# Inverting two blocks of a chunked delta rule as a pair, with their key products issued in the head of the kernel

## The chip, the cores and the metric

The kernel runs on one core of a Trainium2 chip. The metric is device microseconds of one execution; lower is better. The engines are named as the profile names them: PE (TensorE matmul) and PEld (its weight loads), DVE (VectorE), ACT (ScalarE), POOL (GpSimd) and SP (SyncE, which here only issues DMAs).

## The reference, cut to what matters

```python
# q, k, v: (4, 8, 768, 48), beta: (4, 8, 768); all float32
# w_in (384, 2048), w_out (2048, 384): 64-bit floats
k_n = k / (np.linalg.norm(k, axis=-1, keepdims=True) + 1e-06)
state = np.zeros((B, H, D, D))
for t in range(S):                       # S = 768 tokens, one after the other
    kt, vt, bt = k_n[:, :, t], v[:, :, t], beta[:, :, t, None]
    y[:, :, t] = einsum('bhd,bhde->bhe', q[:, :, t], state)
    v_old = einsum('bhde,bhd->bhe', state, kt)
    state = state + bt[:, :, :, None] * einsum('bhd,bhe->bhde', kt, vt - v_old)
x = y.transpose(0, 2, 1, 3).reshape(B * S, H * D)     # 3072 tokens of 384
h = x @ w_in
return np.maximum(0.01 * h, h) @ w_out
```

A recurrence over the tokens (a delta rule, with a 48x48 state per head) is followed by a two-layer feed-forward network on its output.

## The kernel before, in words

The 768 tokens are cut into 12 blocks of 64 (`C`). Within a block the recurrence is solved in closed form: a Gram matrix of the block's keys is made on PE, the inverse of the triangular system that it gives is worked out, and small matmuls with that inverse give the outputs and the new state. All 32 heads of the 4 sequences go together, in two groups `g`.

**The inverse.** `inv` inverts two 32x32 triangles (the halves of a block) per head and sequence on DVE, in 31 elimination steps (`eliminate`, L381): each step is a multiply into `tmp` (L391) and a subtract from `T` (L396), each in two parts `x`, so four instructions and two independent chains. `NB` (L93) says which blocks share one inverse. Blocks 0 and 1 are inverted together, with 128 partitions holding two blocks by two halves by 32 problems (`two`); every later block alone, with the same 64 problems held twice and each copy working on half of the rows of `T`. For a single block, `T` and a transposed copy `Tt` (L456) go to DRAM (`td`, `tt`) and come back as block-diagonal operands `A` and `B` (tile `sq`, L468 and L472) for the products `pz` and `pu` that join the two halves (`merge_z`, `merge_u`).

**The Gram products.** `gram(n)` loads a block's keys and queries (tile `kq`, two buffers), issues on PE products of 64 keys with 64 keys and 64 queries at once (tile `pg`, L308), copies the key part to SBUF on ACT (`gs`), sends it through DRAM (`gd`) into the layout of the inverse (`L`, L346), masks the query part on DVE (L325) and copies the corner of the key part on DVE (`gm`, L333).

**The solve.** `solve(n)` runs through slots: `merge_z`, `merge_u`, `kt` (tile `pk`), `step_w` (`pw`), `step_y` (`py`), the state (`pc`).

**The feed-forward network.** `ffn(n)` has 16 steps `f` per block: a first product (`ph`, L759), an activation on ACT, and a second product into `po` (L750), two steps behind. In block 0 it is one product of float32; from block 1 on in three products of a high and a low part: `xh`, `xl` of its input, `gh`, `gl` of its hidden values (`gl` on DVE, L774), and a high and a low part of the weights.

**The weights** come in as eight pieces `wr` (`load_w`, 1.5 MB each) of 64-bit floats; ACT and DVE make 32-bit floats of them in block 0, from bit fields: `pack` (ACT L152), `conv` (four DVE instructions, L162 to L165), `expand` (ACT L172), `final` (DVE L179). Then `cast` (ACT L186) makes the high part and `lows` (DVE L193) the low part. Piece `j` serves the steps `f` = 2j and 2j + 1. The tiles of pieces 3 and 4 are later those of `A` and `B` (tags c3, c4).

**The order.** The main loop goes block by block and step by step; the tuples `IV`, `GG`, `G4` and `SV` say at which steps of a block the instructions of the inverse, of the Gram products and of the solve for the next blocks are put into the program, and the table `work` does so for the weights. A scheduler then orders each engine's queue at compile time by a model of the times. `behind(name)` keeps an instruction behind a marked one of the same engine. On the chip every queue runs in its fixed order. Block 0's inputs for the solve are fetched by `fetch(0, g)` on SP, between weight pieces 1 and 2; 16 matmuls without use (`warm`, L398) run on PE late in the first inverse.

The lines that place the parts named above:

```python
NB = [[0, 1]] + [[n] for n in range(2, nblk)]                     # L93
for f in range(KA): load_w(f)                                     # L836: pieces 0, 1
for g in range(NGR): fetch(0, g)                                  # L838
for f in range(KA, WEARLY): load_w(f)                             # L840: pieces 2, 3
NF + 0: ((lows, 3),), NF + 1: ((lows, 4),),                       # L875, block 1's steps
NF + 2: ((lows, 5),), NF + 3: ((lows, 6),), NF + 5: ((lows, 7),)  # L876
```

## Time and profile before

| | us |
|---|---|
| median of 3 runs | 609.85 |
| lowest and highest of them | 608.66, 611.44 |
| the profiled execution: its own time | 607.1 |
| its span in the trace | 605.3 |
| PE busy in the span | 564.8 |

The stages can be read from the start of the first `ph` product of each block: the head is 0 to 53.3 us, block 0 is 53.3 to 114.8 us, block 1 is 114.8 to 171.2 us, block 2 is 171.2 to 216.2 us, and a later block takes about 44.2 us. A busy share is an average; what a stage is worth is seen in its own rows, and the wait that ended last there says which engine sets its end.

### The profile page before, as it was taken

Reading aid. Unit: us, or ns where it says so; the run is one execution under the profiler, and the core shown is the slowest. Engines: PE = TensorE matmul, PEld = TensorE weight load, DVE = VectorE, ACT = ScalarE, POOL = GpSimd, SP = SyncE. Lnnn points to the kernel's source line nnn. Section 1 sums busy time; section 2 is a strip of 40 time slices with the busy share of each in tenths; the row PEclk is TensorE's granted clock in tenths of the full one; section 3 lists DMA queues with packets and bytes.
Section 4 is the critical chain, followed back from the end, with each engine's and each line's share of the span. In section 5 each row is a group of like instructions: output and inputs, shape, how many; then the busy total and the mean of one; then the engine's idle time right before and its main releaser. Section 6 shows DMA issues by size and latency. Waiting matters only on the chain.

```text
span 605.3 us, 22381 instructions
## 1 busy us (share of the span) xinstructions
PE 564.8 (93%) x9146; PEld 518.2 (86%) x9146; DVE 448.7 (74%) x1981; ACT 311.3 (51%) x786; POOL 77.8 (13%) x135
## 2 busy tenths in 40 slices
PE   5287989889899999999999999999999999999996
PEld 4266767678799999999999999999999999999996
DVE  3999899978848969859859869769779679341221
ACT  3287976744546446436445445445445445454432
POOL 7000000100140040040130130130120210210100
PEclk9987999999999999999999999999999999999999
DMA  5994942244290273381481490490491450410100
GB/s 124 303 286 174 341 95 60 51 86 83 83 187 8 50 118 109 65 182 32 72 181 23 74 194 9 78 195 16 67 195 29 73 123 2 83 34 3 28 1 27
DMA packets 104423, 59.69 MB, mean 99 GB/s; under 512 B 92544, under 2 KB 93632, under 8 KB 103296
## 3 DMA queue, kind: packets, MB, share of 16 engines
q1 hardware_dynamic: 99168, 50.32, 37.5%
q0 software_dynamic: 4576, 7.22, 5.4%
q8 instruction: 72, 1.18, 0.9%
q10 hardware_dynamic: 576, 0.72, 0.6%
q14 instruction: 31, 0.25, 0.2%
HBM read 46.96 MB, written 11.27 MB: 96 GB/s over the span
## 4 chain that ended last, share of the span: by engine, by line
PE 73%; DVE 16%; DMA 4%; issue 3%; ACT 2%; SPq 1%; DVEq 0%; POOL 0%; ACTq 0%
PE po L750 30%; PE ph L759 29%; DVE tmp L391 3%; DVE T L396 3%; PE pw L656 3%; PE py L693 3%; PE pg L308 2%; DVE w L193 2%; DMA tt<-T 2%; PE pk L631 2%; DVE cg L179 2%; PE pc L631 1%; PE px L728 1%; DVE rq L325 1%; DMA sq<-tt 1%
## 5 line engine op out<-in xcount | busy, mean ns | idle before, releaser
L759 PE MATMUL ph<-xh,w 128*128 128x256 f32 x1056 | 203.9, 284 | 0.0
L750 PE MATMUL po<-w,gh 128*128 128x384 f32 x704 | 180.0, 345 | 0.0
L769 ACT ACTIVATE gh<-ph 128x256 fp32r<-128x256 f32 (+1 forms) x192 | 73.5, 385 | 202.6 <-PE ph L759 121.2
L759 PEld LDWEIGHTS ph<-xh,w 128*128 128x128 f32 x1056 | 168.1, 188 | 2.7 <-issue 2.0
L774 DVE TENSOR_TENSOR gl<-ph,gh 128x256 fp32r<-128x256 f32 x176 | 74.3, 423 | 108.4 <-ACT ph L773 103.3
L759 PE MATMUL ph<-xl,w 128*128 128x256 f32 x528 | 148.4, 283 | 1.8 <-DVE xl L128 1.8
L750 PEld LDWEIGHTS po<-w,gh 128*128 128x128 f32 x704 | 120.2, 188 | 3.7 <-issue 1.4
L750 PE MATMUL po<-w,gl 128*128 128x384 f32 x352 | 112.9, 339 | 2.4 <-DVE gl L774 2.4
L396 DVE TENSOR_TENSOR T<-T,tmp 128x60 f32<-128x60 f32 (+35 forms) x661 | 110.8, 207 | 0.7
L391 DVE TENSOR_TENSOR tmp<-T,L 128x60 f32<-128x60 f32 (+35 forms) x661 | 110.8, 208 | 0.6
L759 PEld LDWEIGHTS ph<-xl,w 128*128 128x128 f32 x528 | 99.5, 188 | 2.6 <-DVE xl L128 2.2
L750 PEld LDWEIGHTS po<-w,gl 128*128 128x128 f32 x352 | 65.3, 188 | 3.2 <-DVE gl L774 3.1
L773 ACT ACTIVATE ph<-ph 128x256 f32<-128x256 f32 x176 | 67.0, 380 | 0.0
L468 POOL DMA_DIRECT2D sq<-tt x32 | 18.9, 596 | 281.3 <-PE po L750 97.9
L801 POOL DMA_DIRECT2D out<-ob x44 | 23.3, 533 | 140.1 <-ACT ob L800 138.1
L325 DVE TENSOR_TENSOR rq<-pg,csb 64x256 f32<-64x256 f32 x80 | 33.7, 422 | 3.0 <-ACT gs L312 1.4
L642 ACT ACTIVATE rt<-pk 48x512 f32<-48x512 f32 x44 | 26.0, 592 | 4.4 <-PE pk L631 3.6
L759 PE MATMUL ph<-x,cg 128*128 128x256 f32 x96 | 22.8, 386 | 4.0 <-DVE cg L179 2.4
L759 PEld LDWEIGHTS ph<-x,cg 128*128 128x128 f32 x96 | 17.7, 190 | 8.9 <-DVE cg L179 4.1
L658 ACT COPY rv<-pw 64x384 f32<-64x384 f32 x48 | 22.7, 474 | 3.6 <-PE pw L656 2.4
L647 DVE TENSOR_TENSOR rv<-rv,nt 64x384 f32<-64x384 f32 x44 | 23.2, 551 | 1.4 <-ACT nt L589 0.6
L693 PEld LDWEIGHTS py<-rv,rq 128*32 128x32 f32 x1536 | 19.4, 114 | 5.6 <-ACT rv L658 2.0
(108 smaller groups left out, 620.8 us busy)
## 6 DMA issues: line engine op xcount, KB each, us to landing
wr<-in_w_all SPq DMA_DIRECT2D x8, 1536.0 KB, 13.4
kq<-in_kqT SPq DMA_DIRECT2D x40, 192.0 KB, 6.7
rk<-in_kv SPq DMA_DIRECT2D x24, 192.0 KB, 5.3
rv<-in_kv SPq DMA_DIRECT2D x24, 192.0 KB, 6.0
rq<-in_qT SPq DMA_DIRECT2D x24, 192.0 KB, 3.4
L<-gd SPq DMA_DIRECT2D x18, 256.0 KB, 4.2
out<-ob POOLq DMA_DIRECT2D x44, 96.0 KB, 5.0
td<-T SPq DMA_DIRECT2D x20, 128.0 KB, 3.3
```

The lines of the kernel that those rows point to most:

```text
L325: nc.vector.tensor_tensor(qa[to, c, b * NPAIR:(b + 1) * NPAIR], pv[b][r, 1], tri[r].rearrange("p (o t) -> p o t", o=1).broadcast_to([C, NP ...
L391: nc.vector.tensor_tensor(tv, t[:, :, j:j + 1].broadcast_to([P, k, w]), L[:, j, j + 1:].rearrange("p (o w) -> p o w", o=1).broadcast_to([P ...
L396: mark["steps"] = nc.vector.tensor_tensor(t, t, tv, ALU.subtract).ins
L642: nc.scalar.mul(ts[g][STATE[g], c], pv[g][c * C:c * C + D].rearrange("p (y v) t -> p y v t", y=2), -1.0)
L647: nc.vector.tensor_tensor(v[to, :, us], v[to, :, us], nt[to, g, :, us].rearrange("p h (u o) -> p h u o", o=1).broadcast_to([C, 2, NPAIR, D ...
L693: nc.tensor.matmul(pv[a:a + HC, u * D:(u + 1) * D], qa[:, c, u, e * HC:(e + 1) * HC], v[:, c, u], start=True, stop=True)
L750: i = nc.tensor.matmul(po[t][:, :DO], a[:, ts_], w, start=(f == 0 and k == 0), stop=(f == NFC - 1 and k + 1 == len(ways)))
L759: i = nc.tensor.matmul(ph, w[:, cc * P:(cc + 1) * P], a, start=(k == 0), stop=(k + 1 == len(ways)))
L769: i = nc.scalar.activation(gh, ph, AF.Prelu, alpha=0.01)
L773: i = nc.scalar.activation(ph, ph, AF.Prelu, alpha=0.01)
L774: mark["gl"] = nc.vector.tensor_tensor(gl, ph, gh.bitcast(F32), ALU.subtract).ins
L801: nc.gpsimd.dma_start(out[r0:r0 + C], ob[a:a + C])
```

## The change

- Blocks 2 and 3 are inverted together, as blocks 0 and 1 are. The 31 steps of this pair are put into block 0 (steps 9 to 17, where block 2's own stood); block 1 gets no inverse.
- The key-with-key products of blocks 2 and 3 (`ahead`) are issued in the head, between the first inverse's preparation and its steps, 64 columns wide. Block 2's keys come with its whole `kq` load, which moves ahead of the weights; block 3's keys alone come by four DMAs on POOL into a corner of the tile of weight piece 7 (`ahead_loads`). ACT copies the products out; 16 DMAs on POOL write `gd` and 8 more write the corner parts to DRAM (`gc`). `arrive`, at step 3 of block 0, reads them back into `L` and `gm` with four DMAs on POOL; the corner copies of DVE are gone for these two blocks.
- The key-with-query products of blocks 2 and 3 and their masks stand in block 1 (steps 4 and 5, and 10 and 11); the masks of block 2 stay behind both chains of the inverse. Block 3's `kq` load stays behind the `B` operand of block 2.
- Block 0's fetches go ahead of all weight pieces; `pack` 0 to 2 stay behind the scaling of block 0's `v`.
- `lows` 3 to 7 go to steps 0, 3, 5, 7, 9 of block 1 in place of 0, 1, 2, 3, 5, and stay behind the last steps of both chains of the pair's inverse (before: behind one of them).
- `A` and `B` of block 3 are filled after block 2's `pu` has read them (`fill`); `T` of a pair goes to DRAM by one DMA per block and array.
- `solve(2)` in block 1 starts at step 7 in place of 4.

```diff
-    NB = [[0, 1]] + [[n] for n in range(2, nblk)]
+    NB = [[0, 1], [2, 3]] + [[n] for n in range(4, nblk)]
...
     def lows(j):
...
-        with behind("dv"), behind("el2" if j > 2 else None):
+        with behind("gl" if j > 3 else "dv"), behind("el0" if j > 2 else None), behind("el1" if j > 2 else None):
             after(nc.vector.tensor_tensor(lo, g, hi.bitcast(F32), ALU.subtract))
...
+    def products(n, g, ps, keys, x, gate=None):
+        w = x.stop - x.start
+        for p in range(NPAIR):
+            for c in range(2):
+                for b in range(2):
+                    r = slice(b * R0, b * R0 + D)
+                    with behind(gate):
+                        nc.tensor.matmul(ps[b][c * 64:(c + 1) * 64, p * w * C:(p + 1) * w * C],
+                                         keys[r, c ^ b, p, 0], kqs[n][g][r, c ^ b, p, x].rearrange("p x t -> p (x t)"),
+                                         start=True, stop=True)
...
+    def ahead_loads():
+        load_kq(pair[0], "kq")
+        t = corner["sb"] = sb.tile([P, 8 * DO], F32, tag="w7", name="k3", bufs=1)
...
+        for g in range(NGR):
+            for b in range(2):
+                nc.gpsimd.dma_start(
+                    keys[b * R0:b * R0 + D, g].rearrange("p s u x t -> p (s u) (x t)"),
+                    kqT[pair[1], g, b].rearrange("d (m x t) -> d m x t", x=2, t=C)[:, :, 0])
+
+    def ahead(n):
...
+        pv = [products(n, g, [t[:, g * h:(g + 1) * h] for t in ps], ks[g], slice(0, 1)) for g in range(NGR)]
...
+        for g in range(NGR):
+            for b in range(2):
+                nc.scalar.copy(gs[:, g, b], pv[g][b][:, 0])
+            grams_out(nc.gpsimd, gd, gs[:, g], g)
+            for c in range(2):
+                nc.gpsimd.dma_start(gc[2 * g + c].rearrange("p u t -> p u t"),
+                                    gs[c * 64:c * 64 + HC, g].rearrange("p b u t -> p (b u) t")[:, :, HC:])
+
+    def arrive():
...
+            nc.gpsimd.dma_start(Lh[b0][i * 64:(i + 1) * 64].rearrange("l j i -> l (j i)"), gd.rearrange("l j i -> l (j i)"))
...
+            nc.gpsimd.dma_start(gm[n], corner[n][1].rearrange("k p u t -> (k p) u t"))
+
+    def gram(n):
+        if n in pair:
+            if n != pair[0]:
+                load_kq(n, "B")
...
+            pv = [products(n, g, [t[:, g * h:(g + 1) * h] for t in ps], kqs[n][g], slice(1, 2), "ph") for g in range(NGR)]
+            for g in range(NGR):
+                masked(n, g, [t[:, 0] for t in pv[g]], *(("el0", "el1") if n == pair[0] else ("gl",)))
+                yield
+            return
...
+                    if two:
+                        nc.scalar.copy(Tt.rearrange("p i (x m) -> p m x i", x=2), T.rearrange("p (m x) i -> p m x i", x=2))
...
+                        if two:
+                            nc.sync.dma_start(tt, Tt[i * 64:i * 64 + HS])
+                            nc.sync.dma_start(rows, T[i * 64:i * 64 + 64])
+                            continue
...
+                    fill(NB[b][0])
...
-                    mark["el2"] = mark["steps"]
+                    mark["el0"], mark["el1"] = mark["step0"], mark["step1"]
...
+            if n == NB[1][0]:
+                fill(NB[1][1])
...
-    for f in range(KA):
-        load_w(f)
     for g in range(NGR):
         fetch(0, g)
-    for f in range(KA, WEARLY):
+    ahead_loads()
+    for f in range(WEARLY):
         load_w(f)
     signs()
     next(fg)
+    weave(1, (iv, 2, 0, 1))
+    for n in pair:
+        ahead(n)
     for j in range(NPACK):
-        pack(j)
-    weave(1, (iv, NI, 0, 1))
+        pack(j, "vs")
+    weave(1, (iv, NI - 2, 0, 1))
...
-        3: ((expand, 3, "h0_3"),),
+        3: ((expand, 3, "h0_3"), (arrive,)),
...
-        NF + 0: ((lows, 3),), NF + 1: ((lows, 4),),
-        NF + 2: ((lows, 5),), NF + 3: ((lows, 6),), NF + 5: ((lows, 7),)}
+        NF + 0: ((lows, 3),), NF + 3: ((lows, 4),),
+        NF + 5: ((lows, 5),), NF + 7: ((lows, 6),), NF + 9: ((lows, 7),)}
...
-IV, GG = ((9, 17), (6, 17), (2, 12), (2, 12)), ((2, 4), (1, 2))
+IV, GG = ((9, 17), (6, 17), (2, 12), (2, 12)), ((4, 5), (10, 11))
...
-SV = (1, 2, 4, 5, 7, 8, 9), (4, 6, 7, 9, 11, 12), (2, 4, 5, 7, 9, 10, 14), (3, 5, 6, 8, 10, 11, 14)
+SV = (1, 2, 4, 5, 7, 8, 9), (7, 8, 9, 11, 13, 14), (2, 4, 5, 7, 9, 10, 14), (3, 5, 6, 8, 10, 11, 14)
```

## Rows read from the trace of the kernel before

**Rows 1.** Busy time by stage: window, then engines, PE clock, DMA share, GB/s.

```profile
37.40:53.30 15.90, 11.93 (x394) 9.93 (x393) 14.74 (x21) 10.55 (x22) 0.00 (x0) 0.68 0.59 124
...
70.00:89.50 19.50, 17.11 (x228) 12.13 (x220) 18.73 (x30) 16.10 (x26) 0.00 (x0) 1.00 0.65 168
89.50:114.80 25.30, 24.18 (x395) 18.04 (x395) 24.91 (x128) 19.66 (x31) 0.00 (x0) 1.00 0.21 50
114.80:129.00 14.20, 10.01 (x114) 8.31 (x113) 14.04 (x32) 6.47 (x17) 2.21 (x4) 1.00 0.25 48
...
150.00:171.20 21.20, 19.21 (x461) 17.64 (x461) 18.21 (x112) 11.73 (x28) 3.54 (x6) 1.00 0.45 97
...
260.80:305.00 44.20, 44.20 (x732) 41.55 (x731) 35.79 (x177) 21.73 (x60) 5.59 (x11) 1.00 0.48 94
```

**Rows 2.** Waits of PE in block 0 (us, times, longest): the longest.

```profile
PE ph L759 <- DVE cg L179: 2.4, 1, 2.4
```

**Rows 3.** Waits of PE in block 1: the three longest.

```profile
PE po L750 <- DVE gl L774: 2.4, 2, 1.4
PE pc L668 <- issue: 1.9, 1, 1.9
PE ph L759 <- DVE xl L128: 1.8, 2, 1.2
```

**Rows 4.** Chain that ended last, block 0: ends of an unbroken DVE stretch.

```profile
70.36 1.76 DVE w L193
...
87.83 1.65 DVE cg L179
```

**Rows 5.** Timeline of DVE: block 2's masks, corners, inverse; low parts of the weights.

```profile
74.22 1.75 DVE L325 TENSOR_TENSOR rq<-pg,csb 64x256 f32<-64x256 f32 x4
...
76.00 0.58 DVE L333 COPY gm<-gs 32x256 f32<-32x256 f32 x2
...
99.93 0.28 DVE L391 TENSOR_TENSOR tmp<-T,L 128x31 f32<-128x31 f32 x2
...
118.95 6.75 DVE L193 TENSOR_TENSOR w<-cg,w 128x1536 fp32r<-128x1536 f32 x4
...
129.66 0.17 DVE L396 TENSOR_TENSOR T<-T,tmp 128x8 f32<-128x8 f32 x1
```

**Rows 6.** Timeline of DVE in the head: first and last step of the first inverse.

```profile
16.79 0.28 DVE L391 TENSOR_TENSOR tmp<-T,L 128x31 f32<-128x31 f32 x2
...
37.14 0.19 DVE L396 TENSOR_TENSOR T<-T,tmp 128x16 f32<-128x16 f32 x1
```

**Rows 7.** Timeline of ACT: scaling of block 0's v; transposed copy of T.

```profile
29.91 7.40 ACT L595 ACTIVATE rv<-rv,nt 64x48 f32<-64x48 f32 x32
...
129.87 1.11 ACT L456 COPY T<-T 128x512 f32<-128x512 f32 x1 [0.30 <-DVE T L396]
```

**Rows 8.** Timeline of PE: small products and the matmuls without use.

```profile
17.18 2.16 PE L264 MATMUL ph<-qx,kx 48*64 48x64 f32 x58
...
31.87 6.72 PE L403 MATMUL warm<-neg 128*128 128x512 f32 x16
...
69.51 1.10 PE L308 MATMUL pg<-kq 48*64 48x128 f32 x32
...
139.92 0.64 PE L501 MATMUL pz<-sq,gm 128*32 128x128 f32 x16 [0.55 <-DMA sq<-tt]
```

**Rows 9.** Chain that ended last, last block: two feed-forward steps without a wait.

```profile
572.29 2.13 PE ph L759 x18
574.42 2.11 PE po L750 x12
```

**Rows 10.** Groups of POOL: DMA issues of the Gram products.

```profile
L316 POOL DMA_DIRECT2D gd<-gs x8 | 4.7, 593 | 50.5 <-ACT gs L312 45.9 <-issue 4.2 <-ACT xh L127 0.4
```

**Rows 11.** The page's groups (busy, mean ns) and DMA issues (us to landing).

```profile
L774 DVE TENSOR_TENSOR gl<-ph,gh 128x256 fp32r<-128x256 f32 x176 | 74.3, 423 | 108.4 <-ACT ph L773 103.3
...
kq<-in_kqT SPq DMA_DIRECT2D x40, 192.0 KB, 6.7
```

More of the change, by code (lines that the diff above doesn't have):

```diff
@@ new lines, in grams_out, with masked @@
+    def grams_out(queue, gd, gs, g):
+        for c in range(2):
+            for e in range(2):
+                a = e * HS + g * GH + c * GU
+                queue.dma_start(
+                    gd[a:a + GU].rearrange("l j i -> j l i"),
+                    gs[c * 64 + e * HC:c * 64 + (e + 1) * HC].rearrange("p b u t -> p (b u) t")[:, :, e * HC:(e + 1) * HC])
+    def masked(n, g, pq, *gates):
+        qa, to = of("q", n, g), DATA[g]
+        for b in range(2):
+            for c in range(2):
+                r = slice(c * 64, (c + 1) * 64)
+                with ExitStack() as gate:
+                    for x in gates:
+                        gate.enter_context(behind(x))
+                    nc.vector.tensor_tensor(
+                        qa[to, c, b * NPAIR:(b + 1) * NPAIR], pq[b][r],
+                        tri[r].rearrange("p (o t) -> p o t", o=1).broadcast_to([C, NPAIR, C]), ALU.mult)
@@ L331, in corners @@
                     k = 2 * g + c
-                    with behind("gl") if n > 2 else nullcontext():
+                    with behind("gl"):
                         nc.vector.tensor_copy(gm[n][k * HC:(k + 1) * HC].rearrange("p (b u) t -> p b u t", b=2), gs[c * 64:c * 64 + HC, :, :, HC:])
-            if n == 2:
-                masked()
-                corners()
-            elif not g:
-                masked()
+            if not g:
+                masks()
                 held.append(corners)
             else:
-                tails.extend([[masked], held + [corners]])
+                tails.extend([[masks], held + [corners]])
                 held.clear()
@@ L394, in eliminate @@
             parts.append((tv, t[:, :, j + 1:]))
-        for tv, t in parts:
-            mark["steps"] = nc.vector.tensor_tensor(t, t, tv, ALU.subtract).ins
+        for x, (tv, t) in enumerate(parts):
+            mark["steps"] = mark[f"step{x}"] = nc.vector.tensor_tensor(t, t, tv, ALU.subtract).ins
     def warm(x, count):
@@ L413, in inv @@
         T = X[:, 0:M * HC].rearrange("p (m i) -> p m i", m=M)
-        if two:
+        if not b:
             nc.gpsimd.memset(T, 0.0)
@@ L485, in place, with fill @@
                 half_of(n, g, e), Tts[n][0][a:a + HC].rearrange("p (y g u) i -> p g y u i", y=2, g=NGR)[:, g])
+    def fill(n):
+        td, tt = Tts[n]
+        A, B = square(0), square(1)
+        queue = nc.gpsimd if n > NS else nc.sync
+        for k in range(4):
+            r = slice(k * HC, (k + 1) * HC)
+            mark["A"] = queue.dma_start(A[r, :, r], tt[k * GU:(k + 1) * GU].rearrange("u i m -> i u m")).ins
+        for v in range(4):
+            r = slice(v * HC, (v + 1) * HC)
+            with behind("A" if n > NS else None):
+                mark["B"] = queue.dma_start(B[r, :, r], td[1, v::4].rearrange("l m i -> m l i")).ins
     squares = {}
```

127 lines of the change are left out of this document (63 added, 64 removed).

## The prediction

> **What bounds the kernel now.** I read the busy time by stage first. From block 3 on PE has no idle time: 44.20 of 44.20 us in the window from 260.8 [rows 1]. Nothing in this change shortens those blocks, so any gain lies before 171 us. There the picture differs. Block 0 lasts 61.5 us, with PE busy 17.11 of 19.50 us and DVE 18.73 in its middle; block 1 lasts 56.4 us (114.8 to 171.2) against 44.2 for a steady one, and PE is busy 10.01 of its first 14.20 us while DVE is busy 14.04 [rows 1].
>
> The waits of PE come next. In block 0 the longest is 2.4 us for the last unpacking of a weight piece on DVE [rows 2]. In block 1 PE waits 2.4 us for `gl`, 1.8 us for `xl`, both made on DVE, and 1.9 us for nothing that the profile shows [rows 3]. The chain of waits and the timeline say what keeps DVE: in block 0 the chain stays on DVE without a break from 70.36 to 89.48 us [rows 4]; at the start of block 1 four low parts of weights run as one piece of 6.75 us at 118.95, ahead of the last steps of block 2's inverse (which end at 129.83) and of the `gl` that PE waits for [rows 5]. So the early blocks hang on DVE, and the question is what DVE loses and gains, and when.
>
> **Block 0, 70 to 89.5 us.** Removed from DVE: the masks of block 2 (two groups at 1.75 us) and its corners (two at 0.58) [rows 5], 4.66 us of the unbroken 19.1 [rows 4]. Removed from PE: two 128-column products at 1.10 us [rows 8], so 17.11 becomes 14.9 us; ACT loses four small copies of its 16.10 [rows 1]. DVE then has 14.5, PE 14.9 and ACT some 15 us of work. At best the 19.5 us shrink by 4.6; at worst by nothing, if PE and ACT then wait for each other. PE's 2.4 us wait is the surest part; with three engines level I take two thirds, **-3.0** (-4.6 to 0).
>
> **Rest of block 0.** PE is busy 24.18 of 25.30 us there [rows 1], and no product leaves it: **0** (-0.5 to 0). DVE does the pair's inverse in this stretch. Its steps cost what those of blocks 0 and 1 do, of the same shapes: 16.79 to 37.33, 20.5 us [rows 6]. They began at 99.93 for block 2 [rows 5]; 3.0 earlier and 0.5 later for a `T` twice as large gives 97.4; with one `final` in between (1.65 [rows 4]), three `xl` and two `gl` (0.42 each [rows 11]) the pair ends at E = 97.4 + 20.5 + 1.7 + 2.1 = 121.7. Block 1 would begin at 114.8 - 3.0 = 111.8.
>
> **Start of block 1.** The low parts now wait for both chains of the inverse, so the burst cannot run ahead of `xl` and `gl`. Of the 4.2 us that PE waited for these [rows 3] only inversion instructions of 0.2 to 0.3 us still stand between: **-3.0** (-4.2 to 0). What is late next is `lows` 3: E + 1.76 [rows 4] = 123.5. Steps 6 and 7 need it, after three pairs of steps of 2.13 + 2.11 us [rows 9], a product of 1.1 and a wait of 1.2: 111.8 + 12.7 + 2.3 = 126.8. Cover 3.3 us; each later piece has 4.2 us more. If the cover is gone, PE waits for the difference.
>
> **Products of queries.** Block 1 issues those of blocks 2 and 3 where it issued one full product of block 3: the same columns in twice as many matmuls, 128 instructions with their halves. By the row of the 128-column form nothing changes; by the row of 64-column products, 2.16 / 58 = 37 ns each, they take 4.8 us in place of 2.2 [rows 8]. That row is from the head; I stay near the form in block 0: **+0.3** (0 to +2.6).
>
> **New waits in block 1.** From the end of block 2's inverse (129.83) to `pz` (139.92) it took 10.1 us [rows 5, 8]. ACT's copy of `T` doubles, +1.1 [rows 7], so `pz` can run at E + 11.2 = 132.9. Its place, step 7, comes at 111.8 + 7 x 2.12 + 2.3 = 128.9. If the queue holds it there, PE stands 4.0 us, with all feed-forward products behind it; before it had come some steps later than written and waited 0.55 [rows 8]. **+0.5** (0 to +4.0). The second is block 4's Gram product at step 13: its keys can load only after block 3's query product at step 10 freed the buffers; 6.7 us to landing [rows 11] against three steps, 6.4 us, of cover: **+0.5** (0 to +3.0, about half of the landing).
>
> **Rest of block 1.** DVE was busy 18.21 of 21.20 us with the second inverse [rows 1], which is gone. Block 1 exceeds a steady block by 12.2; one extra product explains 2.2, the three waits 6.1; the other 4 are small delays behind DVE, ACT and DMA. I take **-1.0** (-2.0 to 0). The 1.9 us without a releaser stays, as I cannot say what ends it: **0** (-1.9 to 0). Block 2: **0** (-0.5 to 0).
>
> **The head.** The key products run where PE is idle, ahead of the 6.72 us of matmuls without use [rows 8]. Those must not end later than 40.2, when the solve's first products start after the transposes; they ended at 38.6, so 1.6 us of cover. They wait for a PSUM buffer that ACT's copies free, behind the scaling of `v`, 7.40 us, which began at 29.91 [rows 7]; the earlier fetch should bring it forward, and if it does not the cover is gone. The clock granted from 37.4 to 53.3 was 0.68 on average, a mix of 1.2 and 2.4 GHz [rows 1]; more PE work before it could shift the change of level. **0** (-1.0 to +1.5). The 24 writes on POOL at 0.593 us [rows 10] are 14.2 us, beside the elimination; `arrive` waits behind them, and so does, by its tile, the DVE instruction that opens weight piece 7, near 63. From 38 at the latest, 52: covered.
>
> Here a page speaks against the change: the Trainium skill, "SBUF — State Buffer", section "SBUF: two separate sides", says that a DMA issued from GpSimd stalls while DVE runs in a mode that takes the shared port, with 620 ns becoming about 3100. The row has 593 ns [rows 10], and DVE was over 80% busy in the stages in which these issues fall [rows 1], so the trace does not show it; the eliminations have two SBUF inputs, which by that page block GpSimd only where it reads SBUF. By the page's slow figure the 24 writes would take an estimated 74 us.
>
> **Sum.** -3.0 - 3.0 + 0.3 + 0.5 + 0.5 - 1.0 = -5.7 us. Against the profiled execution, 607.1 (span 605.3 and 1.8 around it), that is 601.4; the median of the runs was 2.75 higher, 609.85, so the forecast is 604.2. About 0.5% (3 us) is what a measurement tells from no change.
>
> **Rivals.**
> *Both gains in full.* -4.6 in block 0, -4.2 and -1.9 for the waits of block 1 and -1.5 for its rest, +1.3 of new costs: -10.9, 599. For it speaks that block 1 then has no DVE-heavy stretch; against it that three engines are level in block 0.
> *The load only moves.* ACT or PE sets block 0's middle (0), half of the start's waits stay behind inversion steps (-1.5), new costs +1.3: 609.6. For it: the pair's 20.5 us fall in the stretch where DVE was already busy 24.91 of 25.30 [rows 1].
> *Slower: the pair ends too late for its solve.* If `pz` holds PE at step 7, the stall is E + 11.2 - 128.9. At E = 121.7 it is 4.0; the whole gain is lost at E = 123.9 (stall 6.2 where 0.5 was summed), and it is 0.5% slower beyond 126.9. At E = 128.5 the stall is 10.8: +4.6, 614.5. For it: block 2's last steps were pushed back by 11 us [rows 5]; against: what pushed them is now kept behind.
> *POOL held by DVE.* `L` must be there when the inverse's preparation starts, some 9 us ahead of its steps: near 88. With 28 issues from about 38 each may take 1.8 us; at 3 us `L` comes at 122, E moves by 34 to 156, and `lows` 3, needed at 126.8, comes at 157.5: PE stands 31 us, 635. That is what the page's rule would make of it. Against it: 0.593 [rows 10].
>
> **Chances.** Forecast 0.52, both gains in full 0.12, only moved 0.20, late pair 0.11, POOL 0.05. Faster by over 0.5%: 0.50 + 0.12 + 0.05 = 0.67. Within: 0.02 + 0.14 + 0.02 = 0.18. Slower: 0.01 + 0.09 + 0.05 = 0.15. The range 597 to 610.5 leaves out some 0.04 below (all low bounds together) and 0.14 above. The forecast case alone spans 599 to 607.
>
> **What would show it.** Block 0's middle without the 2.4 us wait, and its end near 112; no L193 before the last L396 of the pair, which ends near 122; first `gl` of block 1 within 1 us of its activation; `pz` near 133 with PE waiting under 1 us; block 1 some 52 to 54 us long; the head still 53 us. The prediction is wrong if the head moves by over 1.5 us, if block 1 begins after 114, or if PE waits over 3 us for `pz` or block 4's keys.

## The result and the profile after

The change makes the kernel slower: 618.5 us median (617.8 to 619.9, 4 runs) against 610.6 (4 runs), ratio 1.0133 [1.0096, 1.0171]. The forecast was 604.2. The profiled execution of the changed kernel took 617.8 us and its span is 616.0; that of before took 607.1, with a span of 605.3, so 10.7 us are to be found in the traces. The medians differ by 7.9 only: the profiled execution of before lies 3.5 us under the median of these four runs, and that of the changed kernel is its fastest.

By the stages ("block 1 to its last transposes" ends where PE starts the transposes that close the block): the head ends at 57.4 us (53.3 before), block 0 lasts 68.5 us (61.5), block 1 to its last transposes 54.3 (54.0), block 2 between its transposes 44.3 (44.9). The head costs 4.1, block 0 7.0, block 1 0.3, and block 2 gives 0.6.

Busy time by stage of the changed kernel (window, length; PE, PEld, DVE, ACT, POOL; granted clock, DMA share, GB/s), to be laid beside [rows 1]. The granted clock is the share of full speed, 2.4 GHz, that PE was given; 0.50 is the lower of the two levels, 1.2 GHz.

```profile
57.40:76.00 18.60, 16.44 (x181) 12.31 (x182) 10.94 (x17) 15.46 (x22) 5.50 (x9) 1.00 0.89 311
76.00:92.00 16.00, 8.24 (x21) 5.39 (x19) 11.05 (x16) 5.83 (x8) 3.07 (x5) 0.68 0.51 160
92.00:125.90 33.90, 32.44 (x543) 24.70 (x543) 28.95 (x90) 27.98 (x43) 0.00 (x0) 1.00 0.17 37
125.90:140.00 14.10, 13.24 (x148) 12.38 (x147) 13.45 (x72) 5.25 (x16) 2.15 (x4) 1.00 0.14 30
...
149.00:155.60 6.60, 6.22 (x49) 4.91 (x41) 3.49 (x6) 3.72 (x12) 0.00 (x0) 0.50 0.50 78
```

From 76 to 92 PE is busy half the time, and from 81 to 91 it has the lower clock (0.51). The waits of block 0 say why (engine, line, what was waited for: total, times, longest):

```profile
DVE wr L135 <- DMA gc<-k: 12.1, 1, 12.1
...
PE ph L846 <- DVE cg L179: 10.2, 3, 7.8
```

The memset itself, in DVE's timeline:

```profile
80.68 0.06 DVE L135 MEMSET wr<- 128x1 f32 x1 [12.06 <-DMA gc<-k]
```

DVE stands 12.1 us in front of this one memset of 0.06 us, the one that opens the tile of weight piece 7. The keys of block 3 and the copied products lie in that tile, and the `gc` writes on POOL read it. PE's wait for unpacked weights, 2.4 us before [rows 2], becomes 10.2. POOL's timeline (start, length, instruction; in brackets the idle time before it and what ended it):

```profile
9.54 1.41 POOL L334 DMA_DIRECT2D k<-in_kqT  x2
13.93 0.64 POOL L334 DMA_DIRECT2D k<-in_kqT  x1 [2.98 <-issue]
15.76 0.63 POOL L334 DMA_DIRECT2D k<-in_kqT  x1 [1.19 <-issue]
16.43 0.96 POOL L483 MEMSET T<- 128x1024 f32 x1
17.45 2.08 POOL L114 COPY rk<-csb 64x768 f32<-64x768 f32 x2
36.42 1.75 POOL L309 DMA_DIRECT2D gd<-k  x3 [16.89 <-ACT k L352]
41.99 0.58 POOL L309 DMA_DIRECT2D gd<-k  x1 [3.82 <-issue]
...
48.93 0.59 POOL L309 DMA_DIRECT2D gd<-k  x1 [4.35 <-ACT zs L609]
...
71.26 0.59 POOL L309 DMA_DIRECT2D gd<-k  x1 [2.75 <-issue]
...
78.49 0.57 POOL L355 DMA_DIRECT2D gc<-k  x1 [3.85 <-issue]
```

Each write takes 0.57 to 0.59 us, as in [rows 10], but gaps stand between them, and the last is out at 79.05. The 24 writes that were summed at 14.2 us take 42.6 from the first to the last: some 14 us of issuing, 23.8 us in gaps of up to 3.9 us that the profile calls "issue" (POOL waited for nothing that it shows), and 4.4 us of waiting for ACT.

In the head, DVE's timeline in the changed kernel shows the end of the inverse's preparation, its first step, and the transpose that follows its last:

```profile
17.42 0.20 DVE L491 COPY T<-cb 128x32 f32<-128x32 f32 x1 [2.03 <-POOL T L483]
17.51 2.56 DVE L498 TENSOR_TENSOR L<-L,cb 128x512 f32<-128x512 f32 x2
19.99 0.28 DVE L459 TENSOR_TENSOR tmp<-T,L 128x31 f32<-128x31 f32 x2
...
43.25 2.00 DVE L510 STREAM_TRANSPOSE tc<-T 128x1024 f32<-128x1024 f32 x1
```

and before, with POOL idle, the two multiplies that are at L498 now:

```profile
15.59 1.29 DVE L430 TENSOR_TENSOR L<-L,cb 128x512 f32<-128x512 f32 x2
```

The first step begins at 19.99 in place of 16.79 [rows 6], and from there to the transpose `tc` it takes 23.3 us, not 20.6. Of the late start 1.9 us are waiting: the zeroing of `T` stands on POOL behind four key loads with gaps between them. The other 1.3 are the two multiplies at L498, which take 2.56 us beside POOL's copy and took 1.29 before. So `tc` comes 5.9 us late (43.25, 37.36 before), of which the end of the head shows 4.1. The Trainium skill, "SBUF — State Buffer", section "SBUF: two separate sides", says that a DVE operation with two SBUF inputs and a GpSimd operation that reads SBUF shut each other out of a shared port. The doubling agrees with it.

The slower steps have to do with `warm`, the matmuls without use, as PE's timeline shows:

```profile
27.84 0.44 PE L300 MATMUL pa<-kq 48*64 48x64 f32 x2 [7.13 <-DMA kq<-in_kqT]
...
36.39 0.61 PE L469 MATMUL warm<-T,csb 128*128 128x32 f32 x2 [1.77 <-ACT k L352]
36.81 5.26 PE L471 MATMUL warm<-neg 128*128 128x512 f32 x16
```

The prediction had asked that `warm` end by 40.2 us; it ends at 42.1. Its first matmul reads `T`, so DVE may not overwrite that part of `T` until it has run, and it stands on PE behind the early key products, which wait 7.1 us for their keys. DVE shows no wait in the steps, but from 35.1 to 38.2 us and again from 39.7 on its queue holds the instructions of one of the two chains alone.

Block 1 is almost as long in both kernels, with different waits. Its windows, first before, then in the changed kernel (PE's busy time follows the length; the granted clock is the third number from the end):

```profile
114.80:168.80 54.00, 47.28 (x779) 42.92 (x778) 45.46 (x199) 27.53 (x70) 3.98 (x7) 1.00 0.43 88
```

```profile
125.90:180.00 54.10, 48.78 (x841) 44.64 (x840) 38.43 (x116) 25.58 (x63) 5.55 (x10) 0.94 0.47 98
```

PE's waits in block 1 of the changed kernel, against [rows 3]:

```profile
PE pz L585 <- DMA sq<-tt: 1.9, 1, 1.9
PE pg L300 <- issue: 1.4, 1, 1.4
PE ph L846 <- DVE xl L128: 0.9, 2, 0.7
PE pg L300 <- DMA kq<-in_kqT: 0.8, 1, 0.8
PE pu L585 <- ACT ph L860: 0.4, 1, 0.4
```

The wait for `gl` is gone and that for `xl` halved, as forecast. The new wait for `pz` is followed by 6.6 us at the lower clock, 0.50 in the row from 149 to 155.6 above; before, the clock was 1.00 in every 5 us of block 1.

### The profile page after: what moved, and what is told of

Read it like the earlier page. It is cut to its first block, busy times and chain, and to the rows that moved or that the text cites. A ratio compares the mean times of both kernels' runs of the same rounds, so it can differ in the third digit from the quotient of the medians.

```text
span 616.0 us, 22511 instructions
## 1 busy us (share of the span) xinstructions
PE 569.9 (93%) x9274; PEld 524.1 (85%) x9274; DVE 435.9 (71%) x1837; ACT 311.3 (51%) x783; POOL 98.4 (16%) x167
## 4 chain that ended last, share of the span: by engine, by line
PE 74%; DVE 9%; issue 6%; POOL 4%; DMA 2%; SPq 2%; ACT 2%; DVEq 0%; POOLq 0%; ACTq 0%
PE ph L846 30%; PE po L837 30%; DVE T L464 3%; DVE tmp L459 3%; PE pg L300 3%; PE pw L743 2%; PE py L780 2%; PE pk L718 2%; POOL gd L309 1%; DMA sq<-td 1%; PE pc L718 1%; PE px L815 1%; DMA kq<-in_kqT 1%; PE pu L585 1%; DVE cg L179 1%
## 5 line engine op out<-in xcount | busy, mean ns | idle before, releaser
L464 DVE TENSOR_TENSOR T<-T,tmp 128x16 f32<-128x16 f32 (+14 forms) x602 | 104.3, 212 | 1.0
L459 DVE TENSOR_TENSOR tmp<-T,L 128x16 f32<-128x16 f32 (+14 forms) x602 | 104.3, 212 | 0.9
L846 PE MATMUL ph<-x,cg 128*128 128x256 f32 x96 | 25.6, 419 | 11.7 <-DVE cg L179 10.2
L846 PEld LDWEIGHTS ph<-x,cg 128*128 128x128 f32 x96 | 19.2, 207 | 16.5 <-DVE cg L179 11.3
L128 DVE TENSOR_TENSOR xl<-px,xh 128x256 fp32r<-128x256 f32 x33 | 13.1, 421 | 14.5 <-ACT xh L127 14.5
```

Of the source, the lines that this page charges most:

```text
L459: nc.vector.tensor_tensor(tv, t[:, :, j:j + 1].broadcast_to([P, k, w]), L[:, j, j + 1:].rearrange("p (o w) -> p o w", o=1).broadcast_to([P ...
L464: mark["steps"] = mark[f"step{x}"] = nc.vector.tensor_tensor(t, t, tv, ALU.subtract).ins
L846: i = nc.tensor.matmul(ph, w[:, cc * P:(cc + 1) * P], a, start=(k == 0), stop=(k + 1 == len(ways)))
```

## The experiments

All runs, with the stages in us (block 1 to its last transposes). Each stage figure is from one profiled execution, while the times of one kernel spread over several us: `warm` freed, for one, ran in 606.3 to 613.0. So a stage tells where time went, and whether a kernel is faster is told by the ratio, which is to runs of before beside it (their medians are 609.3 to 610.6). An interval that holds 1 tells no change.

| kernel | median | ratio to before, interval | head | block 0 | block 1 |
|---|---|---|---|---|---|
| before | 609.85 | | 53.3 | 61.5 | 54.0 |
| changed | 618.5 | 1.0133 [1.0096, 1.0171] | 57.4 | 68.5 | 54.3 |
| piece 7 late | 607.7 | 0.9968 [0.9938, 0.9998] | 57.7 | 57.5 | 54.1 |
| writes on SP | 617.62 | 1.0123 [1.0081, 1.0166] | 56.9 | 64.7 | 54.8 |
| twice the room on POOL | 609.73 | 1.0001 [0.9977, 1.0025] | 57.0 | 57.4 | 56.3 |
| before, twice the room | 610.82 | 1.0003 [0.997, 1.0035] | 53.9 | 61.8 | 54.3 |
| key loads on SP | 617.28 | 1.0113 [1.0051, 1.0176] | 56.4 | 67.7 | 54.1 |
| packs behind the copies | 617.01 | 1.0097 [1.0058, 1.0135] | 58.4 | 66.0 | 56.7 |
| `warm` freed | 610.6 | 1.0012 [0.9983, 1.004] | 57.6 | 57.7 | 58.6 |
| head's cures together | 610.05 | 1.0009 [0.9976, 1.0041] | 54.8 | 58.0 | 56.8 |
| weights first | 622.63 | 1.0183 [1.0137, 1.023] | 71.8 | 57.8 | 55.0 |
| before, low parts spread | 609.58 | 1.0012 [0.9983, 1.0041] | 54.5 | 61.7 | 50.4 |
| the same, gated | 613.41 | 1.0048 [1.0023, 1.0072] | 54.8 | 62.7 | 55.0 |
| fillers | 608.63 | 0.9981 [0.9949, 1.0013] | 57.6 | 58.1 | 54.0 |
| solve and masks late | 653.26 | 1.069 [1.0629, 1.0751] | 58.0 | 57.7 | 59.2 |
| the same, twice the room, `warm` freed | 645.51 | 1.0554 [1.0494, 1.0615] | 58.3 | 59.9 | 62.1 |
| block 1 a step later | 610.66 | 1.0014 [0.9985, 1.0043] | 57.8 | 57.5 | 56.2 |
| the same, twice the room | 608.96 | 0.9985 [0.9958, 1.0011] | 58.2 | 57.1 | 56.8 |
| block 3's keys on POOL | 611.66 | 1.0029 [0.9999, 1.006] | 56.7 | 57.8 | 59.3 |
| all cures | 611.15 | 1.003 [0.9997, 1.0062] | 57.3 | 58.0 | 55.3 |

### The writes on POOL

**Piece 7 late.**

```diff
-        4: ((load_w, 7, "dv"), (conv, 4), ...
-        7: ((expand, 5, "h0_7"), ...
+        4: ((conv, 4), ...
+        7: ((load_w, 7, "dv"), (expand, 5, "h0_7"), ...
```

> The load of weight piece 7, with the DVE instruction that opens its tile, stands at step 7 of block 0 in place of step 4; nothing else differs from the changed kernel (618.5). Theory A, DVE's wait of 12.1 us for the last corner write on POOL is the main loss: the wait falls under 3 us, PE's wait of 7.8 us and the half-clock stretch behind it go, and the kernel takes 607 to 611. Rival B, block 0 is as long without the wait because DVE and ACT are loaded as much: 615 or more.

Theory A holds. Block 0 falls from 68.5 to 57.5 us, and the time by 10.8 us. DVE's longest wait from 50 to 126 us is now

```profile
DVE cg L162 <- ACT cg L152: 3.9, 4, 1.7
```

though POOL's last write issues as late as before this edit:

```profile
78.84 0.57 POOL L355 DMA_DIRECT2D gc<-k  x1 [1.31 <-issue]
```

The memset behind the writes was the cost. Against before, the head now costs 4.4 us, block 0 gives 4.0, block 1 is even (+0.1) and block 2 gives 0.7: together about nothing, and the interval of the ratio only just leaves out 1.

**Writes on SP** (`gd`, `gc`, `L` and `gm` issued by `nc.sync`).

> All writes and reads of the early Gram products (gd, gc, L, gm) are issued on SP in place of POOL; piece 7 stays at step 4. Theory A, the POOL queue itself paces the 24 writes: on SP they are out by 60 us, the wait of DVE for piece 7 is under 1 us, 607 to 611. Rival C, the DMA engines are too busy with the weights, whichever queue issues: the last write lands after 70 us, DVE still waits 4 us or more, 613 or more.

Theory A holds for the writes and not for the time; rival C has the time and not the cause. The writes are out by 61.6 us and DVE no longer waits for them. But weight pieces that issued at 59.05 in the changed kernel stand behind them on SP, and DVE waits 11.5 us in all, 8.1 at the longest, for ACT's packs of these. SP's timeline in this kernel:

```profile
65.87 1.77 SPq L137 DMA_DIRECT2D wr<-in_w_all  x3
```

**Twice the room on POOL.** No row shows what the setting holds; I call it the room of POOL's queue. `gl` loses a buffer to make place for it.

```diff
-dynamic_dma_scratch_size=1024
+dynamic_dma_scratch_size=2048
-tag="gl", ..., bufs=3
+tag="gl", ..., bufs=2
```

> The changed kernel with dynamic_dma_scratch_size 2048 in place of 1024, so that POOL's queue can hold twice as many descriptors, and with two buffers of gl in place of three to make room for it (a cost of its own in blocks 1 and later). Theory A (POOL's 24 writes are paced by the room in its queue: bursts of about three, then gaps of 1 to 4 us): the last of the writes issues at 60 to 70 us in place of 79.1, DVE's wait for the memset of weight piece 7 falls from 12.1 to under 4 us, block 0 lasts 59 to 62 us in place of 68.5; time 609 to 614, by what gl costs. Rival B (DVE's or ACT's work holds POOL's issues): gaps and the wait are as in the changed kernel, 616 to 621. Rival C (the writes are paced by how fast the 16 DMA engines move 128-byte pieces): the bursts get longer but the last write still ends near 79.

POOL's timeline in this kernel:

```profile
9.54 2.66 POOL L334 DMA_DIRECT2D k<-in_kqT  x4
12.24 0.96 POOL L483 MEMSET T<- 128x1024 f32 x1
...
36.57 2.35 POOL L309 DMA_DIRECT2D gd<-k  x4 [21.61 <-ACT k L352]
38.91 1.15 POOL L355 DMA_DIRECT2D gc<-k  x2
...
54.76 1.42 POOL L355 DMA_DIRECT2D gc<-k  x2
```

The key loads issue without a gap and the zeroing of `T` comes 4.2 us earlier. The writes take 19.6 us, with 4.4 us of "issue" left of 23.8, and are out at 56 in place of 79, earlier even than theory A had it. DVE's wait is gone, and block 0 is as short as with piece 7 late. So theory A holds: the gaps go with the setting. The third buffer of `gl` has no part in those of the key loads, which stand ahead of any `gl`. DVE did not cause the gaps either: in the changed kernel two of them end at 71.26 and 78.49, and DVE was idle from 68.6 to 80.7. In block 1 PE now waits 3.5 us for `gl`. The lost buffer may be the reason why the time is 2 us over that of piece 7 late; no run separates the two.

**Before, twice the room** (`dynamic_dma_scratch_size` 2048, `ys` with two buffers).

> The kernel before with dynamic_dma_scratch_size 2048 and two buffers of ys in place of three. Theory A (the room in POOL's queue matters for the change, not for the kernel before, where eight writes of block 4 wait for nothing that is late): POOL's eight writes at 164 issue within 5 us in place of 9.4, DVE's wait for L in block 2 (3.6 us) shortens, time 608 to 611. Rival B (two buffers of ys cost): over 611. Rival C (the shorter wait for L is worth time): under 607.

Theory A holds: seven of eight writes issue in 4.1 us and DVE's wait for `L` in block 2 is gone, but the time stays. In the profiled execution (613.2 us) block 2 even took 50.0 us in place of 44.9; `pz` there waited 2.57 us for its DMA. The room gains time in the changed kernel and none in the kernel before.

### The head

**Key loads on SP** (four `k3` loads by `nc.sync`).

> The four loads of block 3's keys are issued on SP in place of POOL. Theory A, the first inverse starts 3.2 us late because the memset of T and the copy of identities stand behind these loads on POOL: its first step goes back from 20.0 to about 17 us, and the head's end by 2 to 3 us; 615 to 617. Rival D, the head's end is set by the matmuls without use and ACT, not by the start: the head's end moves under 1 us; 618.

DVE's timeline in this kernel:

```profile
11.82 1.94 DVE L250 STREAM_TRANSPOSE L<-S 128x1024 f32<-128x1024 f32 x1
...
17.18 1.29 DVE L498 TENSOR_TENSOR L<-L,cb 128x512 f32<-128x512 f32 x2
```

L498 takes 1.29 us again. From the making of `L` to the first step it takes 6.6 us as before, and 9.8 in the changed kernel, so all of the 3.2 us goes with these loads on POOL. But the edit has a price of its own: `L` is made 1.6 us later (11.82; 10.19 in the changed kernel, 10.20 before). The only other kernel with these loads on SP has 11.83, and the rest lie at 9.9 to 10.7. The loads now issue ahead, at 1.66 us, and the DMA share from 4 to 8 us is 1.26 in place of 0.47. So the head ends only 1.0 us earlier, where theory A had 2 to 3. DVE's wait for the writes stays, at 12.7 us, and the time hardly moves.

**Packs behind the copies** (`pack` 0 to 2 behind ACT's copies of the products).

> The three early weight unpackings on ACT are kept behind ACT's copies of the early Gram products. Theory A, one chain of the first inverse waits for the matmuls without use, these for a PSUM buffer, and it for ACT, which stands in front of a weight piece that has not landed: the steps of the first inverse take 20.5 to 21.5 us in place of 23.2, 615 to 617. Rival D, the products themselves come too late for that: the steps take over 22.5 us; 618.

Theory A falls and rival D holds: the steps still take 24.0 us. PE's key products wait 7.0 us for `kq`, and the first matmul of `warm`, which reads `T`, stands behind them.

**`warm` freed** (with piece 7 late).

```diff
-                warm(T[:, 0], WARM[j])
+                warm(eye[:, 0:HC], WARM[j])
```

> Two edits against the changed kernel: weight piece 7 is loaded at step 7 of block 0, as in the run before that took this out (607.7 us), and the first matmul of the head's matmuls without use reads a constant in place of T, so that no subtraction of the elimination has to wait for it. Theory A (the elimination's one chain stands still behind that matmul, which is late behind the key products): the elimination's steps in the head, 23.2 us from the first to the end in the changed kernel and 20.5 before, take 20.5 to 21.5, the first product of block 0 starts near 55, and the time is 605 to 606. Rival B (the steps are slow because POOL's DMA issues or ACT's copies disturb DVE): the steps stay at 23, time 607 to 608.5. Rival C (the steps get faster but the head's end is set by PE's clock or by the queue of ACT): steps near 21, first product still at 57, time 607 to 608.5.

The steps take 20.3 us, so theory A holds for them: `warm` was what held them up. Yet the head ends at 57.6, which is rival C, though the time is 2 us over its 607 to 608.5. ACT's timeline shows what is late next:

```profile
42.52 1.62 ACT L152 COPY cg<-wr 128x1536 bf16<-128x1536 bf16 x1 [1.79 <-DMA wr<-in_w_all]
44.02 0.67 ACT L352 COPY k<-pa 128x256 f32<-128x256 f32 x2
44.71 1.26 ACT L555 COPY rt<-tc 32x512 f32<-32x512 f32 x2
```

`tc` was made by 42.3, but the copy of it that `pz` needs stands behind a pack of a late weight piece.

**Head's cures together** (`warm` freed, key loads on SP, squares zeroed by POOL, piece 7 late).

> The last kernel with two edits more: the four loads of the keys of block 3 issue from SP in place of POOL (which freed POOL for the zeroing of T: first step 18.4 in place of 20.0 in the run that did this alone), and the two square tiles of the pair are zeroed by POOL in place of ACT, where they stood ahead of the activations of block 1. Theory A (head 0's rest and block 1's `pz` wait hang on these): 602.5 to 605, PE's wait for `pz` in block 1 falls from 1.5 to 1.9 us to under 1 and the head ends 1.5 us earlier than in the run beside it. Rival B (block 1's wait is that of the DMAs from T to the square tiles, not of the zeroing): `pz` still waits 1.5 us or more, only the head gains: 604 to 606. Rival C (the loads on SP hold the loads of block 0's inputs and of the weights up, and the head gains nothing): 606 to 608.

The head ends at 54.8, 1.5 us over before. Here too the key loads on SP make `L` 1.6 us late (11.83). With that taken off, which is an estimate, the causes found make up the whole 4.1. The time gains nothing and lies outside what all three theories had (602.5 to 608). `pz` still waits 1.6 us, as rival B had it, block 1 is 2.7 us longer than with piece 7 late alone, as PE waits 2.6 us there for block 3's keys (0.8 with piece 7 late), and a later `pu` waited 2.5 us for a square.

**Weights first** (piece 7 late; the four pieces ahead of block 0's inputs and the keys).

> The changed kernel with weight piece 7 late, and with the loads on SP in the order of before: the first four weight pieces ahead of block 0's inputs and of block 2's keys. Theory A (the head is paced by the 16 DMA engines, busy at a share of 1.0 to 46 us, and the keys now stand ahead of weights whose pieces ACT waits for): packs 0 to 2 on ACT start earlier, but the keys land 5 us later, PE's pa and the matmuls without use behind them too, and the elimination stands still longer: first product of block 0 at 58.5 to 62, time 609 to 613. Rival B (the order hardly matters, the sum of bytes does): first product at 57 to 58.5, time 606.5 to 608.5.

Theory A holds in its mechanism, but its head (58.5 to 62) and its time (609 to 613) are far exceeded: 71.8 and 622.6. The keys land last of all, at 47.7 us (30.4 in the changed kernel), `warm` stands behind their products, and the elimination behind `warm` (DVE's timeline):

```profile
52.63 0.27 DVE L464 TENSOR_TENSOR T<-T,tmp 128x110 f32<-128x110 f32 x1 [13.32 <-PE warm L469]
```

The DMA share from 14 to 44 us is 1.02 in this kernel, in the changed one and before, at 298 to 301 GB/s: the loads that the change puts into the head come on top of DMA engines that were full.

### Block 1

**Before, low parts spread** (steps 0, 3, 5, 7, 9, behind both chains; the later ones' gate on `gl` left out).

> The kernel before with one part of the change alone: the low parts 3 to 7 of the weights wait for both chains of block 2's inverse and are spread over block 1 (steps 0, 3, 5, 7, 9 in place of 0, 1, 2, 3, 5). Theory A (this part, and not the pair, gives the 3 us at the start of block 1): PE's waits there for gl (2.4) and xl (1.8) fall to under 1.5 us together, time 606 to 607.5. Rival B (without the pair DVE's second inverse in block 1 takes what is gained): the start's waits fall but cg, masks or gl wait later in block 1, time 609 to 611. Rival C (wo low parts come late for the products that read them): PE waits for L193's lows over 1.5 us in block 1, time 611 to 614.

Without the gate all five low parts ran as one piece of 8.43 us and PE waited 3.2 us for `gl`, so this is not the part as the change has it. Still block 1 took 50.4 us, 3.5 less; block 2 then took 49.4, 4.5 more, where DVE waited 6.2 us for block 4's `L`, whose writes on POOL had not moved.

**The same, gated** (`behind("gl" if j > 3 else "dv")` added).

> The kernel before with the low parts 3 to 7 gated and spread exactly as in the change: in the earlier run of this part the four later ones lacked their wait for the last gl, and all five ran as one piece of 8.43 us at 119.19, ahead of a gl that PE then waited 3.2 us for. Theory A (this part gives the start of block 1 what was forecast): no piece of low parts over 3.5 us, PE's waits for gl and xl at the start of block 1 under 1.5 us together in place of 4.2, block 1 50 to 51.5 us to its last transposes in place of 54.0, time 606 to 607.5. Rival B (block 2 gives it back: POOL's writes of block 4's corners, whose L came at 184 with block 1 3.5 us shorter too, do not move): DVE waits 6 us for L in block 2, block 2 lasts 47 to 49.5 us in place of 44.9, time 608.5 to 610.5.

The waits at the start fall to 0.4 us, as theory A had it, but block 1 does not get shorter, and neither theory names what follows: `pu` waits 6.4 us. The `sq` loads that it needs issued at 138.00 before and still issue at 137.54, behind writes and key loads, while PE comes for them earlier. Block 2 takes 49.1 us, as rival B had it, though DVE waits 2.9 us for `L` there and not 6. By its ratio this part alone makes the kernel before slower by some 0.5%. PE's timeline:

```profile
144.01 1.08 PE L501 MATMUL pu<-sq,zs 128*32 128x128 f32 x16 [6.38 <-DMA sq<-td]
```

**Fillers** (piece 7 late; four matmuls of 128 by 512 before `pz` and three before `pu`, read by nothing).

> The changed kernel with weight piece 7 late and with matmuls that nothing reads put into block 1: four of 128 by 512 ahead of block 2's pz (some 1.7 us by the row of those in the head) and three ahead of its pu (1.3). Theory A (the price of the dry spell at pz is mostly the halved clock that follows it, 7 us at half speed): the clock stays over 0.9 from 136 to 150, and although PE gets 3 us more work the time is that without them or less: 604.5 to 607.5. Rival B (the clock does not hang on that spell): the clock falls to 0.5 for 5 us or more all the same, time 608 to 611.

The scheduler put the first four at 131.4 us, ahead of the dry spell (the stretch in which PE waits for `pz`), so the spell was not filled. The time lies in rival B's range, and block 1 is as long as without the fillers. The clock was still low for part of 140 to 145 (0.68, where theory A had over 0.9), and had been 0.50 from 139 to 145 with piece 7 late. The run decides little.

**Solve and masks late** (`SV[1]` 8, 9, 10, 12, 14, 15; `GG` 8, 9).

> The changed kernel with weight piece 7 late (607.7 us by itself) and, in block 1, block 2's query products and masks issued at steps 8 and 9 in place of 4 and 5, and the steps of block 2's solve one later (8, 9, 10, 12, 14, 15). Theory A (PE runs dry at `pz` because low parts, masks, the copy of T and the DMAs to the squares all fall right behind the pair's inverse, and the dry spell halves the clock for some 6 us): PE's waits for pz and pu in block 1, 2.5 us in the kernel without this edit, fall under 0.8, the clock stays over 0.95 in every 5 us of block 1 where it was 0.50 for 7, block 1 lasts 50 to 52 us to its last transposes in place of 54.1, time 603 to 605.5. Rival B (the wait only moves to py and px at the end of block 1, since the solve ends one step later): block 1 stays at 53 to 55, time 607 to 609. Rival C (the clock falls anyway): waits gone, clock 0.5 for 5 us or more, time 605 to 607.

This layout does not do what it was meant to do: block 4's Gram step at 13 asks for the `y` of step 14, so the solve is pulled a step ahead in the later blocks, of which most take 48 to 52 us in place of 44.2. The run tells nothing of block 1. A second kernel had the same layout with twice the room (`ys` with two buffers) and `warm` freed, and piece 7 in its old place. For it 599 to 603 us were expected, or 604 to 608 if block 1 gave nothing; it took 645.5, with later blocks as long, so it tells nothing of block 1 either.

**Block 1 a step later** (piece 7 late; `SV[1]` 8, 9, 10, 12, 13, 14; `GG` 6, 7).

> The changed kernel with weight piece 7 late and block 1 laid out a step later, this time without pulling the solve forward: block 2's query products at steps 6 and 7, its solve at steps 8, 9, 10, 12, 13, 14 (the earlier try had the step that gives y at 14, behind block 4's Gram products at 13 that ask for it, so the solve ran a step ahead of its plan in every later block, and these took 48 to 52 us). Theory A (PE runs dry at pz because the DMAs from T to the squares land some 8 us behind the pair's inverse, and the dry spell halves the clock): waits for pz and pu under 0.8 us, clock over 0.9 in every 5 us of block 1, block 1 50 to 52.5 us to its last transposes in place of 54.1, time 603.5 to 606. Rival B (with pz later PE waits for gl or lows there): the same dry spell under another name, time 607 to 609.

The wait for `pz` falls to 0.2 us and the clock stays at 1.00 to 150. Then PE waits 3.2 us in all for block 3's keys, which stand last on SP behind the DMAs of the inverse. PE's timeline:

```profile
148.89 0.29 PE L300 MATMUL pg<-kq 48*64 48x64 f32 x2 [1.94 <-DMA kq<-in_kqT]
149.88 0.69 PE L300 MATMUL pg<-kq 48*64 48x64 f32 x30 [0.69 <-DMA kq<-in_kqT]
```

and the windows of this kernel, the clock third from the end:

```profile
145.00:150.00 5.00, 2.37 (x81) 2.01 (x82) 2.58 (x6) 3.02 (x6) 0.00 (x0) 1.00 0.81 171
150.00:158.00 8.00, 7.41 (x146) 6.55 (x148) 4.23 (x10) 1.32 (x4) 0.00 (x0) 0.57 0.41 107
```

This is rival B's outcome, the same dry spell under another name, though it had named `gl` or the low parts as the new wait and not the keys.

**The same, twice the room** (`ys` with two buffers; piece 7 in its old place).

> The change with dynamic_dma_scratch_size 2048 (two buffers of ys in place of three) and block 1 a step later as in the run beside it; weight piece 7 where the change has it. Theory A (two independent costs): POOL's writes out by 58 us, head to the first product 57, block 0 57 to 59.5 us, block 1 50 to 52.5, time 601 to 605. Rival B (only the ring pays): 606 to 610.

Rival B holds: only the room pays.

**Block 3's keys on POOL** (to block 1 a step later).

```diff
-                load_kq(n, "B")
+                load_kq(n, "kq", nc.gpsimd)
```

> The changed kernel with weight piece 7 late and block 1 a step later, as in the run before (610.7 us: no wait for pz any more, but four waits of 3.2 us in all for block 3's keys at 147 to 151.5, and the clock at half for some 6 us behind them), and the four loads of block 3's keys issued from POOL, which is idle there, as soon as the buffers are free, in place of SP, where they stand behind 22 DMAs of the inverse's results. Theory A (block 1 is held by one serial queue: whatever stands last on SP behind the inverse's end makes PE run dry, and the clock falls): no wait of PE for kq of block 3, clock over 0.9 in every 5 us of block 1, block 1 50 to 52.5 us to its last transposes in place of 56.2, time 603.5 to 606.5. Rival B (a third wait takes the place, for example block 4's keys or the issue wait at 163): block 1 stays over 53.5, time 607 to 610.

Theory A falls, and rival B holds in that a third wait takes the place, in a time slightly above its own. No wait for these keys is left, but they now cross the inverse's DMAs (share 1.05 from 135 to 140), and `pz` waits longer than in any other run: 5.0 us, 0.2 without this edit. PE's timeline, and the windows:

```profile
141.84 1.08 PE L585 MATMUL pz<-sq,gm 128*32 128x128 f32 x16 [4.96 <-DMA sq<-tt]
```

```profile
140.00:148.00 8.00, 6.16 (x39) 5.74 (x40) 3.11 (x4) 1.03 (x4) 0.00 (x0) 0.59 0.55 57
```

**All cures** (the same, `warm` freed, twice the room, piece 7 in its old place).

> The change with dynamic_dma_scratch_size 2048 (two buffers of ys), the head's matmuls without use reading a constant, block 1 a step later and block 3's keys from POOL. Theory A (all three causes are cured at once): first product of block 0 at 55 to 57, block 0 57 to 60, block 1 50 to 52.5 to its last transposes, time 600 to 604. Rival B (the head or block 1 gives it back): 605 to 609.

Rival B, and worse: the head ends at 57.3, `pz` waits 3.3 us, block 1 takes 55.3. The version with piece 7 late alone has the lowest median, 0.3% under before, but its interval reaches 0.9998 and overlaps those of the fillers and of both kernels with twice the room and the change's piece 7, so that it is the best of these is not shown.

## Why the prediction was wrong

- **Failed step: "the 24 writes on POOL ... are 14.2 us ... From 38 at the latest, 52: covered."** The dependence was named (`arrive` and the memset of piece 7 wait behind them), but the writes were sized by their issue time, without the gaps. They took 42.6 us: 14 of issuing, 23.8 of gaps "issue" and 4.4 of waiting for ACT. The memset waited 12.1, and that is 10.8 us of time (piece 7 late). The row was there: in [rows 10] eight issues of 0.593 us carry 4.2 us of idle time "issue". The rival of POOL held by DVE rightly had the writes slow, and nothing else of it came: its price was 3 us a write, and 42.6 / 24 is 1.8, the pace that it called harmless; its place was `L`, which was in time; its cause was DVE, and the gaps go with more room, two of them standing where DVE is idle.
- **The head, 0 (-1.0 to +1.5): +4.1.** What was missed is order: `T`'s zeroing and the copy on POOL, behind and beside the key loads (first step 3.2 later), `warm` behind the key products on PE and so DVE behind the keys' landing (2.7), and keys ahead of weights on full DMA engines (the third weight piece lands at 41.9 us, 36.4 before). The condition was written down, `warm` to end by 40.2, and it failed by 1.9 us. With the first two cured and the squares off ACT the head is within 1.5 us of that of before, about as much as that cure makes `L` late (head's cures together).
- **Block 0's middle, -3.0:** the size is right once the wait for the writes is gone: with piece 7 late block 0 as a whole gives 4.0 (61.5 to 57.5), near the bound of 4.6. The part called surest gave little: the one wait of 2.4 us for the last unpacking became three of up to 0.8, 2.2 in all. PE's waits in block 0 fell from 5.1 to 3.8 us and its busy time from 56.8 to 54.1, so most of the gain is the products that left.
- **Block 1's start, -3.0:** right: the waits for `gl` and `xl` fell from 4.2 to 0.9.
- **The rest of block 1:** summed, with the start, to -2.7; measured +0.3. The `pz` term (0.5) was 2.3 with `pu`; block 4's keys (0.5) were in time, block 3's 0.8 late, unforeseen. The clock behind the dry spell was in no term: an estimate from 6.6 us at half speed is a loss of 3.3, about the 3.0 that lack, but no run took the fall of the clock away by itself. Before, 6.7 us of idle time (54.0 - 47.3 busy), in pieces of up to 1.9 us, did not lower the clock in block 1; now 5.3 (54.1 - 48.8) do. In before with twice the room, with waits there of the same sizes (2.4 us for `gl` in two, 1.8 for `xl`), it did fall (0.70 from 130 to 135 us). Which spells lower it is not settled.
- **The pair's inverse:** its steps take what was summed (24.1 us with piece 7 late, 24.3 forecast), but begin 47.6 us into block 0, not 44.1, and so end 14.2 us into block 1, not 9.9. The rival of the late pair thus had half of its condition; `pz` came 8.6 us after the end of the steps (11.2 summed) and held PE for 1.9 us only.
- **Sum by what was measured:** head +4.1, block 0 +7.0, block 1 +0.3, block 2 -0.6: +10.8, span +10.7. Two of the three signs of being wrong came: the head moved by over 1.5 us, and block 1 began at 125.9, after 114.

Everything of the pair (results, squares, block 3's keys) must cross the DMA queues between the inverse's end and the solve. That this is what keeps block 1 from its gain fits four layouts that each only moved the wait; none of them isolates it. Why PE has some 1 to 2 us of "issue" before `pg` in nearly all of them stays open. No layout of the change was found in which block 1 keeps its gain; that there is none is not shown.

## What to carry to other kernels

A queue's transfers are sized from the start of the first to the end of the last, gaps included; look in the rows of before for "issue" idle beside the issue time, and ask which tile the last of them still holds. Loads that are moved into a stage where the DMA share is 1.0 compete with all that is loaded there (here the third weight piece landed 5.5 us later), and through queues in order (`warm` on PE, the zeroing on POOL) they can hold up engines that have no part in it. A wait saved at one end of a block is a gain only if the work it held back can be used: here it met results that come at their own time, and a dry spell of PE of some 2 us then cost an estimated 3 more in clock.

## What was not expected of the hardware

- POOL's DMA issues of 0.58 us came in groups of one to three with gaps of up to 3.9 us between them, 23.8 us in all; with one setting at 2048 in place of 1024, 4.4 us were left.
- Two multiplies of DVE took 2.56 us beside a POOL copy, and 1.29 without it; with twice the room, where POOL's memset and copy come earlier, two small operations on 32 columns took 0.83 and 0.85 in place of 0.19 and 0.18.
- Waits of PE of 1.6 to 6.4 us were followed by 3 to 7 us at a granted clock of 0.50, 1.2 GHz, in block 1 of several of these kernels; in before itself, pieces of up to 1.9 us in block 1 were not. The Trainium skill, "TensorE: Matmul & The Clock Gate", section "Part 1: The HAM clock gate (the "warmup" mystery)", has waits for DMAs lower the clock to 1.2 GHz; the rows agree.
